# Splitting the first batch's keys and values by heads in an attention-plus-FFN kernel

## The chip, the cores and the metric

The kernel runs on one core of one Trainium2 chip. The metric is the device time of one execution in microseconds (us); the median of three runs before the change is 248.95 us (248.72 to 249.54). The traced execution of the same kernel spans 246.9 us from its first to its last instruction, and all times inside it below are counted from its start. Engines are named as in the profile: PE is the matrix engine (PEld its weight loads), DVE the vector engine, ACT the scalar engine, POOL the general-purpose engine that also issues most of the DMA transfers here, SP the engine that issues the others.

## The reference

A linear attention with cosine weights is followed by a feed-forward network with a product of two branches. There are 8 batches, 8 heads, 576 positions and a head dimension of 64:

```python
theta = pi / 2 * arange(576) / 576
phi(x) = concat([relu(x) * cos(theta), relu(x) * sin(theta)], axis=-1)     # 128 features
kv  = einsum('bhsf,bhsd->bhfd', phi(k), v)       # 128 x 64 for each head
z   = sum over s of phi(k)
num = einsum('bhsf,bhfd->bhsd', phi(q), kv)
den = einsum('bhsf,bhf->bhs', phi(q), z) + 1e-6
x   = (num / den), heads side by side            # 4608 tokens x 512
out = ((x @ w1) * (x @ w2)) @ w3 @ w_out         # 512 -> 1024 -> 1024 -> 512
```

All inputs and the output are 32-bit floats in DRAM; inside, the matrix products take bfloat16 operands and accumulate in 32 bits.

## The kernel before, in words

The product `w3 @ w_out` does not depend on the tokens, so the kernel forms it once (`w34b`, 1024 x 512) and then needs only three products for each token. Tokens are worked off in nine tiles of 512 columns. `ffn_groups(t)` is a generator that issues the matrix products of tile t in small groups and yields after each; after every yield the main loop runs whatever is listed in `slots[g]`, and so attention work of later batches is woven between the groups by hand. Nothing is moved by a scheduler (`tc.manual_schedule()`)[...].

The start is written out ahead of the loop, because nothing is there yet to be overlapped. For batch 0:

1. SP loads k as 32-bit floats (`load_first`, `load_first4` for the last 64 positions, "chunk 4"). POOL loads v, then q in two halves of two position chunks each, then the first column blocks of w1 and w2 (256 of 1024 columns a time, `load_w12`), casting to bfloat16 on the way. At most eight transfers of POOL's are under way: the ninth waits for the first one's completion.
2. DVE computes the cos and sin tables (`_trig_tables`), then the cos features of k in five chunks of positions; ACT computes the sin features; DVE copies v into `va`, whose last column is 1, so that the denominator comes out of the same product.
3. PE runs 27 products of zeros (`idle_mms`) while it waits, then `kv_first`: 40 products of 128 x 65, heads 0 to 3 in one PSUM bank, 4 to 7 in another. ACT copies both to `kvs`.
4. For a chunk c of 128 positions, `q_tr` turns the features of q on PE, ACT or DVE copies them out of PSUM (`qpT`), `num(0, c)` multiplies with `kvs`, DVE divides (`den`, `xblk`), `x_tr` turns the result on PE and DVE or ACT copies it into the columns of `xT` for tile 0. Chunks 0 and 1 are so treated ahead of the loop, chunks 2 and 3 from slots 1 and 3.

Tile 0 of the FFN begins as soon as chunk 0 is in `xT`. `on_half` treats columns 0 to 255, then 256 to 511; within a half, `pair` 0 and 1 are the hidden blocks 0-1 and 2-3 of w1 and w2. For `pair` 0 of half 0 and for all of half 1 the products are cut to 128 columns ("quarters"), so that they can begin before the second chunk of a half is there. `multiply` copies the w1 branch out of PSUM on ACT (`asb`) and multiplies it with the w2 branch on DVE (`abT`). Hidden blocks 4 to 7 follow with 512 columns each. Each block needs two PSUM banks out of four (`ffn_tile`, two pools of two).

Then come, still in tile 0, 16 groups that form `w34b`: for each 128-row block jp of w3, `w3_tr(jp)` turns it on PE, DVE copies it (`w3T`), and `w34_mm(jp, 0)` and `w34_mm(jp, 1)` multiply it with the first and second half of w_out. The order on PE around the first block is: `w3_tr(0)` (slot 13), hidden block 7, `w34_mm(0, 0)`, `w3_tr(1)` (slot 16), `w34_mm(0, 1)`. The weights for it are loaded by `other_loads`, which POOL begins once chunk 0's `xblk` is written: w2 and w1's remaining columns, w3 row block 0, w_out half 0, w3 block 1, w_out half 1, w3 blocks 2, 3, 4-5, then k of batch 1 and w3 blocks 6-7.

In the names of the profile, L462 is every product of `products` (the FFN's first layer), L532 the second layer, L237 `w34_mm`, L225 `w3_tr`, L336 and L349 turns of q, L417 `x_tr`, L365 `num`, L322 `kv_first`, L186 the products of zeros, L467/L468 `multiply`, L515/L519 the same for whole blocks.

Of the kernel before, what the change touches and what calls it, by code (L numbers as in the profile page):

```python
# [68 lines left out]
def kernel(  # L69
# [29 lines left out]
                                            space=bass.MemoryType.PSUM))  # L99
    first = [ctx.enter_context(ExitStack()) for _ in range(2)]  # L100
    ps_idle = first[1].enter_context(tc.tile_pool(name="ps_idle", bufs=1, space=bass.MemoryType.PSUM))
    ps_first = first[0].enter_context(tc.tile_pool(name="ps_first", bufs=1, space=bass.MemoryType.PSUM))

# [32 lines left out]
    def load_first4(eng, t, src, b=0):  # L136
        eng.dma_start(out=t[0:64, :, 4, :], in_=src[b, :, 512:S, :].rearrange("h p d -> p h d"))
# [16 lines left out]

    k0 = raw[0, "k"] = wst.tile([P, H, NCH, D], FP32, name="kf")
    q0 = raw[0, "q"] = ld.tile([P, H, NCH, D], BF16, name="qs", bufs=2)
    v0 = raw[0, "v"] = ld.tile([P, H, NCH, D], BF16, name="vs")
    load_first(nc.sync, k0, k)
    load_first4(nc.sync, k0, k)
    load_first(nc.gpsimd, v0, v)  # L160
    zeros = const.tile([P, 512], BF16, name="zeros")
    nc.vector.memset(zeros[:], 0.0)
    va_bufs, kp_bufs, qp_bufs = [], [], []

    def feature_buffers(i):

        va = const.tile([P, NCH, H, D + 2], BF16, name=f"va{i}")
        nc.vector.memset(va[:, :, :, D:D + 1], 1.0)
        nc.vector.memset(va[64:128, 4, :, 0:D], 0.0)
        va_bufs.append(va)  # L170
        for name, bufs in (("kp", kp_bufs), ("qp", qp_bufs)):
            fp = const.tile([P, NCH, H, F], BF16, name=f"{name}{i}")
            nc.vector.memset(fp[64:128, 4, :, :], 0.0)
            bufs.append(fp)

    feature_buffers(0)
    tiny = const.tile([P, 1], FP32, name="tiny")
    nc.scalar.activation(out=tiny[:], in_=zeros[:, 0:1], func=ACTF.Relu, scale=1.0, bias=0.0)

    unread = ps_idle.tile([P, 512], FP32, name="unread")  # L180
    kva = ps_idle.tile([P, 512], FP32, name="kva")

# [4 lines left out]

    idle_mms(27)
    cosv, sinv = _trig_tables(nc, const)
    identb = const.tile([P, P], BF16, name="identb")  # L190
    load_first4(nc.gpsimd, v0, v)
    load_first(nc.gpsimd, q0, q, 0, 2)
    make_identity(nc, identb[:])
    load_first(nc.gpsimd, q0, q, 2, 2)
    def load_w12(c0, n):
# [4 lines left out]
    load_w12(256, 256)  # L200
    load_first4(nc.gpsimd, q0, q)
    nc.gpsimd.dma_start(out=w1b[:, :, ds(512, 256)], in_=w1v[:, :, ds(512, 256)])

    def other_loads(behind):

        seen = sm.tile([P, 1], BF16, name="seen", bufs=1)
        nc.gpsimd.tensor_copy(out=seen[:], in_=behind)
        nc.gpsimd.dma_start(out=w2b[:, :, ds(512, 256)], in_=w2v[:, :, ds(512, 256)])
        load_w12(768, 256)
        for jp in range(2):  # L210
            load_w3(jp, 1)
            load_wout(jp)
        for jp in range(2, 4):
            load_w3(jp, 1)
        load_w3(4, 2)
        load(1, "k")
        load_w3(6, 2)
# [95 lines left out]

    def kv_first():

        kp, qp, va = feat[0]
        kvs = sm.tile([P, H, D + 1], BF16, name="kvs", bufs=2)
        kvb = ps_att.tile([P, 2, 512], FP32, name="pnum")
        halves = (kva[:, :], kvb[:, 0, :])
        for c in range(NCH):  # L320
            for h in range(H):
                nc.tensor.matmul(halves[h // 4][:, ds((h % 4) * 65, 65)], lhsT=kp[:, c, h, :],  # L322
                                 rhs=va[:, c, h, 0:D + 1], start=(c == 0 and h % 4 == 0),
                                 stop=(c == NCH - 1 and h % 4 == 3))
        att_of(0)["kvs"] = kvs
        yield
        for half in range(2):
            nc.scalar.copy(out=kvs[:, 4 * half:4 * half + 4, :], in_=halves[half][:, 0:260])
        yield

# [22 lines left out]
    def num(b, c, chain=True, in_two=False):  # L353
# [3 lines left out]
        qpT, kvs = att[b]["qpT"], att[b]["kvs"]  # L357
        if b == 0 and c == 0:
            nt = ps_first.tile([P, 2, 512], FP32, name="pfirst")
        else:  # L360
            pool = more_att[0] if more_att and order_of(b).index(c) % 2 == 0 else ps_att
            nt = None if in_two else pool.tile([P, 2, 512], FP32, name="pnum")
        banks = [ffn_tile(), ffn_tile()] if in_two else [nt[:, g, :] for g in range(2)]
# [92 lines left out]
    def ffn_groups(t):  # L456
# [14 lines left out]

        def on_half(half):

            if half == 1 and t == 0:
                banks = [(ffn_tile(), ffn_tile()) for _ in range(2)]
                for quarter in range(2):
                    for pair, (a, b) in enumerate(banks):
                        for i in range(2):
                            for ps, w in ((a, w1b), (b, w2b)):
                                products(ps[:, ds(256 * i + 128 * quarter, 128)], w, 2 * pair + i,  # L480
                                         ds(256 + 128 * quarter, 128))
                        if quarter == 1:
                            multiply(a, b, pair, half)
                        if quarter == 0 or pair == 1:
                            yield
                return
            for pair in range(2):
                a, b = ffn_tile(), ffn_tile()
                if pair == 0 and t == 0:
                    for quarter in range(2):  # L490
                        for i in range(2):
                            for ps, w in ((a, w1b), (b, w2b)):
                                products(ps[:, ds(256 * i + 128 * quarter, 128)], w, i,
                                         ds(256 * half + 128 * quarter, 128))
                            if half == 0 and quarter == 0 and i == 0:
                                yield
                        if quarter == 0:
                            yield
                else:
                    for ps, w in ((a, w1b), (b, w2b)):  # L500
                        for i in range(2):
                            products(ps[:, ts(i, 256)], w, 2 * pair + i, ts(half, 256))
                        if w is w1b and (t == 1 or half == 0):
                            yield
                multiply(a, b, pair, half)
                yield

        if t < 2:
            yield from on_half(0)
            yield from on_half(1)  # L510
        for jc in range(4 if t < 2 else 0, 8):
            aT = ffn_tile()
            products(aT[:, :], w1b, jc, slice(0, 512))
            asb = fsb.tile([P, 512], BF16, name="asb")
            nc.scalar.copy(out=asb[:], in_=aT[:, :])  # L515
            yield
            bT = ffn_tile()
            products(bT[:, :], w2b, jc, slice(0, 512))
            nc.vector.tensor_mul(out=abT[:, jc, :], in0=asb[:], in1=bT[:, :])  # L519
            yield  # L520
        if t == 0:
            for jp in range(8):
# [65 lines left out]

    for c in range(NCH):
        prep_k(0, c)  # L590
    for c in range(NCH):
        prep_v(0, c)
    kv_steps = kv_first()
    next(kv_steps)
    q0f = feat[0][1]
    features(0, q0f, q0, 0, scalar_heads=4)
    next(kv_steps)
    prep_q(0, 1)
    idle_mms(2)
    q_tr_halves(0, 0)  # L600
    prep_q(0, 2)
    idle_mms(1)
    num(0, 0)
    q_tr(0, 1, evac=False)[1]()
    other_loads(att[0]["x"][0][:, 0, 0, 0:1])
    features(0, q0f, q0, 3, sin=False)
    features(0, q0f, q0, 3, cos=False)
    idle_mms(2)
    x_tr(0, 0, by_vector=True)
    num(0, 1)  # L610
    q_tr(0, 2, evac=False)[1]()
    ps_ffn = []
    for stack in first:
        stack.close()
    for i in range(2):
        ps_ffn.append(ctx.enter_context(tc.tile_pool(name=f"ps_ffn{len(ps_ffn)}", bufs=2,
                                                     space=bass.MemoryType.PSUM)))


    at(1, lambda: x_tr(0, 1, by_vector=True), lambda: q_tr(0, 3, evac=False)[1](), lambda: num(0, 2))  # L620
    at(3, lambda: x_tr(0, 2), lambda: num(0, 3))
    at(5, lambda: x_tr(0, 3))
    at(6, lambda: features(0, q0f, q0, 4))
    at(23, lambda: transpose_q(0, 4))
# [72 lines left out]
```

## Time and profile before

| | |
|---|---|
| median of 3 runs | 248.95 us (248.72 to 249.54) |
| traced span | 246.9 us |
| PE busy | 240.5 us, 97% of the span |
| DVE, ACT, POOL busy | 135.9, 130.2, 93.4 us |
| DMA moved | 41.22 MB, mean 167 GB/s |
| waits of PE over 0.1 us after 1.2 us | five, together some 2 us, all before 34.1 us |

PE is busy in nearly every slice, so the span is PE's work plus the time in which PE has nothing useful to do. Such time lies only at the start: up to 10.11 us PE runs products of zeros or waits, and from there to 16 us it is used in part. To read the start, the timeline of single engines is more use than the sums: in it, each row has the start, the duration and, in brackets, the idle time before it and what ended that. A product's duration includes its drain, so products that follow one another without a gap overlap in the table by about 0.17 us.

### The profile page before, as it was taken

How to read it: one execution, taken by the hardware profiler on the slowest of the kernel's cores; microseconds unless marked ns; L12 is line 12 of the kernel's file. 1: busy time of each engine (PE TensorE's matmuls, PEld its weight loads, DVE VectorE, ACT ScalarE, POOL GpSimd, SP SyncE). 2: the span in 40 equal slices, each digit the busy share in tenths (PEclk: the TensorE clock that was granted, in tenths of full speed). 3: DMA queues.
4: the chain of work that ended last, by engine and by line, in shares of the span. 5: the costliest groups of instructions: out<-in, count | busy, mean ns of one | idle time of the engine just before them, and what ended most of it. 6: DMA issues, size and time to landing. Idle time of an engine off the chain costs nothing.

```text
span 246.9 us, 5034 instructions
## 1 busy us (share of the span) xinstructions
PE 240.5 (97%) x1872; PEld 130.4 (53%) x1872; DVE 135.9 (55%) x336; ACT 130.2 (53%) x266; POOL 93.4 (38%) x196
## 2 busy tenths in 40 slices
PE   8799999999999999999999999999999999999994
PEld 3479545566975445444544555454545554444443
DVE  7775652668968445647566475547464645312420
ACT  2676313767943873466556654854575333434332
POOL 7654342024512261127032612173322005978700
PEclk9999999999999999999999999999999999999999
DMA  7999999999999969999999999999994536998823
GB/s 199 178 194 199 201 207 204 198 181 173 153 162 142 167 100 149 132 149 134 169 144 155 118 180 150 150 140 140 166 142 89 94 64 214 260 281 289 282 101 128
DMA packets 86200, 41.22 MB, mean 167 GB/s; under 512 B 53792, under 2 KB 82720, under 8 KB 86176
## 3 DMA queue, kind: packets, MB, share of 16 engines
q0 software_dynamic: 37008, 27.20, 71.8%
q1 hardware_dynamic: 49168, 13.71, 35.9%
q8 instruction: 14, 0.23, 0.4%
q14 instruction: 10, 0.08, 0.1%
HBM read 38.80 MB, written 9.44 MB: 195 GB/s over the span
## 4 chain that ended last, share of the span: by engine, by line
PE 85%; DMA 10%; POOL 3%; issue 1%; ACT 0%; POOLq 0%
PE ffnps L462 45%; PE ffnps L532 24%; PE ffnps L237 6%; DMA woutb<-in_moe_w_out_dram 5%; DMA w2b<-in_moe_w_dram 5%; PE pnum L365 4%; PE pnum L305 4%; PE pst L225 1%; PE ffnps L548 1%; POOL qs L133 1%; POOL w1b L196 1%; PE pst L336 1%; POOL vs L133 0%; PE pst L417 0%; POOL w2b L197 0%
## 5 line engine op out<-in xcount | busy, mean ns | idle before, releaser
L462 PE MATMUL ffnps<-xT,w2b 128*128 128x512 bf16 (+2 forms) x344 | 75.5, 344 | 0.0
L462 PE MATMUL ffnps<-xT,w1b 128*128 128x512 bf16 (+2 forms) x344 | 75.5, 344 | 0.0
L519 DVE TENSOR_TENSOR abT<-asb,ffnps 128x512 bf16<-128x512 bf16 x64 | 43.9, 686 | 54.3 <-PE ffnps L462 52.4
L532 PE MATMUL ffnps<-w34b,abT 128*128 128x512 bf16 x280 | 65.0, 379 | 0.0
L515 ACT CAST asb<-ffnps 128x512 bf16<-128x512 f32 x64 | 37.4, 584 | 50.0 <-PE ffnps L462 45.2
L462 PEld LDWEIGHTS <-w2b 128*128 128x128 bf16 x344 | 31.0, 98 | 27.3
L462 PEld LDWEIGHTS <-w1b 128*128 128x128 bf16 x344 | 30.8, 98 | 25.9
L567 POOL COPY seen<-mark 1x1 bf16<-1x1 bf16 x50 | 8.9, 178 | 84.4 <-ACT mark L565 84.4
L532 PEld LDWEIGHTS <-abT 128*128 128x128 bf16 x280 | 26.0, 98 | 27.9 <-DVE abT L519 0.2
L539 ACT COPY osb<-ffnps 128x512 f32<-128x512 f32 x35 | 20.5, 584 | 35.2 <-PE ffnps L532 35.1
L274 ACT ACTIVATE qp<-qs,sinv 128x512 bf16<-128x512 bf16 (+2 forms) x40 | 28.1, 714 | 1.8 <-DMA qs<-in_q_dram 1.8
L383 DVE TENSOR_TENSOR xblk<-pnum,den 128x512 bf16<-128x512 f32 (+1 forms) x37 | 25.6, 691 | 1.3
L297 POOL COPY va<-vs 128x512 bf16<-128x512 bf16 (+1 forms) x30 | 17.6, 621 | 22.9 <-DMA vs<-in_v_dram 22.4
L274 ACT ACTIVATE kp<-ks,sinv 128x512 bf16<-128x512 bf16 (+1 forms) x35 | 25.0, 717 | 0.9 <-DMA ks<-in_k_dram 0.9
L447 POOL DMA_DIRECT2D out_dram<-osb x42 | 22.1, 531 | 2.7 <-issue 2.1
L365 PEld LDWEIGHTS <-qpT 128*128 128x128 bf16 x320 | 15.4, 98 | 8.7 <-DVE qpT L350 0.6
L381 DVE TENSOR_SCALAR den<-pnum 128x8 f32<-128x8 f32 (+1 forms) x37 | 6.0, 163 | 22.6 <-PE pnum L365 22.5
L237 PE MATMUL ffnps<-woutb,w3T 128*128 128x512 bf16 x64 | 15.8, 380 | 0.2 <-DMA woutb<-in_moe_w_out_dram 0.2
L365 PE MATMUL pnum<-kvs,qpT 128*128 128x65 bf16 x296 | 15.8, 194 | 0.0
L270 DVE TENSOR_SCALAR qp<-qs,cosv 128x512 bf16<-128x512 bf16 (+1 forms) x40 | 15.3, 389 | 0.7 <-DMA qs<-in_q_dram 0.7
L305 PEld LDWEIGHTS <-kp 128*128 128x128 bf16 x280 | 11.4, 98 | 4.1
L270 DVE TENSOR_SCALAR kp<-ks,cosv 128x512 bf16<-128x512 bf16 (+1 forms) x35 | 12.5, 367 | 0.0
(88 smaller groups left out, 181.6 us busy)
## 6 DMA issues: line engine op xcount, KB each, us to landing
out_dram<-osb POOLq DMA_DIRECT2D x16, 256.0 KB, 4.5
out_dram<-osb POOLq DMA_DIRECT2D x24, 128.0 KB, 3.9
qs<-in_q_dram POOLq DMA_DIRECT2D x8, 256.0 KB, 7.6
ks<-in_k_dram POOLq DMA_DIRECT2D x6, 320.0 KB, 6.3
qs<-in_q_dram POOLq DMA_DIRECT2D x6, 320.0 KB, 5.9
vs<-in_v_dram POOLq DMA_DIRECT2D x6, 320.0 KB, 5.7
ks<-in_k_dram POOLq DMA_DIRECT2D x6, 256.0 KB, 7.0
vs<-in_v_dram POOLq DMA_DIRECT2D x6, 256.0 KB, 5.4
```

The lines of the kernel that those rows point to most:

```text
L237: nc.tensor.matmul(acc[:, :], lhsT=w3T[:, lc, :], rhs=woutb[:, lc, :], start=(lc == 0), stop=(lc == 7))
L270: nc.vector.tensor_scalar(out=dst[:R, c, :, 0:D], in0=src[:R, :, c, :], scalar1=0.0, scalar2=cosv[:R, at:at + 1], op0=ALU.max, op1=ALU.mult)
L274: nc.scalar.activation(out=dst[:R, c, 0:n, D:F], in_=src[:R, 0:n, c, :], func=ACTF.Relu, scale=sinv[:R, at:at + 1], bias=0.0)
L305: nc.tensor.matmul(kvt[:, h // 4, ds((h % 4) * 65, 65)], lhsT=kp[:, c, h, :], rhs=va[:, c, h, 0:D + 1], start=(i == 0 and h % 4 == 0), sto ...
L365: nc.tensor.matmul(banks[h // 4][:, ds((h % 4) * 65, 65)], lhsT=qpT[:, h, ds(at, 128)], rhs=kvs[:, h, :], start=True, stop=True)
L383: nc.vector.tensor_tensor(out=xblk[rows, g], in0=n4[:, :, :, 0:D], in1=den[rows, g].unsqueeze(3).to_broadcast([R, G, 4, D]), op=ALU.mult)
L447: eng.dma_start(out=rows[:, :, cols], in_=osb[64 * i:64 * i + rows.shape[0], :, cols])
L462: nc.tensor.matmul(out, lhsT=w[:, kc, ts(jc, 128)], rhs=x[:, kc, tok], start=(kc == 0), stop=(kc == 3))
L515: nc.scalar.copy(out=asb[:], in_=aT[:, :])
L519: nc.vector.tensor_mul(out=abT[:, jc, :], in0=asb[:], in1=bT[:, :])
L532: nc.tensor.matmul(ops[:, :], lhsT=abT[:, jc, ts(ms, 128)], rhs=w34b[:, jc, :], start=(jc == 0), stop=(jc == 7))
L539: nc.scalar.copy(out=osb[:, ms % 2, :], in_=ops[:, :])
```

## The change

The idea is to let the first work begin on half of the data. k and v of batch 0 are loaded by halves of the heads; the features, the `kv` product, its copy and the numerator of chunks 0 and 1 are then done for heads 0-3 while heads 4-7 are still on their way. In order:

- k's heads 0-3 are loaded by SP as 32-bit floats, k's chunk 4 into a tile of its own (`k4`); k's heads 4-7 by POOL, cast to bfloat16. v is loaded in two halves by POOL, the second after k's second half. The integer tables for cos and sin go ahead of POOL's first transfer.
- The zero fills of `kp` and `va` for the missing 64 rows go from DVE to ACT; that of `qp` is put off to slot 6.
- `kv_first` is replaced by `first_kv(half)`, `num(0, 0)` and `num(0, 1)` by `first_num(c, half)`. 17 products of zeros stay of 27, and two of the later five.
- Tile 0 of the FFN no longer goes half by half but chunk by chunk for hidden blocks 0-1 (`chunk`), with blocks 2-3 of the first half between chunks 2 and 3, and of the second half after block 4 (`first_tile`). `x_tr(0, 2)` is moved to slot 2, `num(0, 2)` to slot 0.
- In `other_loads` both halves of w_out go ahead of w3 block 1, and q's chunk 4 is loaded after it, where before it went ahead of w1's third block.

The diff, cut to what bears on the order of work:

```diff
-    load_first(nc.sync, k0, k)
-    load_first4(nc.sync, k0, k)
-    load_first(nc.gpsimd, v0, v)
+    load_half(nc.sync, k0[0], k, 0, slice(0, 4))
+    nc.sync.dma_start(out=k4[0:64, :, :], in_=k[0, :, 512:S, :].rearrange("h p d -> p h d"))
...
+    cosv, sinv = _trig_tables(nc, const)
+    load_half(nc.gpsimd, v0, v, 0, slice(0, 4))
...
-    idle_mms(27)
-    cosv, sinv = _trig_tables(nc, const)
-    identb = const.tile([P, P], BF16, name="identb")
+    idle_mms(17)
     load_first4(nc.gpsimd, v0, v)
     load_first(nc.gpsimd, q0, q, 0, 2)
+    load_half(nc.gpsimd, k0[1], k, 1, slice(0, 4))
+    identb = const.tile([P, P], BF16, name="identb")
     make_identity(nc, identb[:])
+    load_half(nc.gpsimd, v0, v, 1, slice(4, 8))
     load_first(nc.gpsimd, q0, q, 2, 2)
...
     load_w12(256, 256)
-    load_first4(nc.gpsimd, q0, q)
     nc.gpsimd.dma_start(out=w1b[:, :, ds(512, 256)], in_=w1v[:, :, ds(512, 256)])
...
-        for jp in range(2):
-            load_w3(jp, 1)
-            load_wout(jp)
+        load_w3(0, 1)
+        for half in range(2):
+            load_wout(half)
+        load_w3(1, 1)
+        load_first4(nc.gpsimd, q0, q)
...
+        def first_tile():
+            banks = [(ffn_tile(), ffn_tile()) for _ in range(2)]
+            for c in range(4):
+                if c == 3:
+                    yield from on_half(0, 1)
+                yield from chunk(*banks[c // 2], c)
+                if c % 2:
+                    multiply(*banks[c // 2], 0, c // 2)
+                yield
+            yield from whole(4)
+            yield from on_half(1, 1)
...
+    first_keys(0)
+    first_values(0)
+    first_kv(0)
     q0f = feat[0][1]
-    features(0, q0f, q0, 0, scalar_heads=4)
-    next(kv_steps)
+    prep_q(0, 0)
     prep_q(0, 1)
     idle_mms(2)
     q_tr_halves(0, 0)
-    prep_q(0, 2)
-    idle_mms(1)
-    num(0, 0)
+    first_keys(1)
+    halves = [first_num(0, 0)]
     q_tr(0, 1, evac=False)[1]()
-    other_loads(att[0]["x"][0][:, 0, 0, 0:1])
...
+    first_values(1)
+    halves[0]()
+    features(0, q0f, q0, 2, sin=False)
+    first_kv(1)
+    halves.append(first_num(1, 0))
+    halves.append(first_num(0, 1))
+    halves[1]()
+    halves[2]()
+    features(0, q0f, q0, 2, cos=False)
+    q_tr(0, 2, evac=False)[1]()
+    other_loads(att[0]["kvs"][:, 4, 0:1])
+    halves.append(first_num(1, 1))
+    x_tr(0, 0, by_vector=True)
+    halves[3]()
...
-    at(1, lambda: x_tr(0, 1, by_vector=True), lambda: q_tr(0, 3, evac=False)[1](), lambda: num(0, 2))
-    at(3, lambda: x_tr(0, 2), lambda: num(0, 3))
-    at(5, lambda: x_tr(0, 3))
-    at(6, lambda: features(0, q0f, q0, 4))
+    at(0, lambda: num(0, 2))
+    at(1, lambda: x_tr(0, 1), lambda: q_tr(0, 3, evac=False)[1]())
+    at(2, lambda: x_tr(0, 2, by_vector=True), lambda: num(0, 3))
+    at(4, lambda: x_tr(0, 3))
+    at(6, lambda: nc.vector.memset(qp_bufs[0][64:128, 4, :, :], 0.0))
+    at(19, lambda: features(0, q0f, q0, 4))
```

The changed kernel has the same 40 slots in tile 0, so everything from slot 7 on, and all of tiles 1 to 8, is issued in the order of before.

## The prediction

> **What bounds the kernel now.** I read the page first, then the waits of PE, then PE's timeline from 0 to 36 us, then the DMA issues one by one, and last the chain of waits.
>
> ```profile
> PE 240.5 (97%) x1872; PEld 130.4 (53%) x1872; DVE 135.9 (55%) x336; ACT 130.2 (53%) x266; POOL 93.4 (38%) x196
> PE   8799999999999999999999999999999999999994
> DMA  7999999999999969999999999999994536998823
> ```
>
> PE is busy everywhere but at the start, and DMA is full from the start to about 85 us. Only the start can give time, and there PE and DMA both have a claim. PE's timeline (start, duration, what it did; overlapping durations mean no gap):
>
> ```profile
> 1.20 7.74 PE L186 MATMUL unread<-zeros 128*128 128x512 bf16 x27 [1.20 <-DVE zeros L162]
> 10.11 0.29 PE L322 MATMUL kva<-va,kp 128*128 128x65 bf16 x4 [1.18 <-DVE va L297]
> ...
> 15.01 0.40 PE L417 MATMUL pst<-identb,xblk 128*128 128x128 bf16 x4 [0.34 <-DVE xblk L383]
> 15.34 0.43 PE L365 MATMUL pnum<-kvs,qpT 128*128 128x65 bf16 x8
> 15.61 0.61 PE L336 MATMUL pst<-identb,qp 128*128 128x128 bf16 x8
> 16.05 0.39 PE L462 MATMUL ffnps<-xT,w1b 128*128 128x128 bf16 x4
> 16.27 0.39 PE L462 MATMUL ffnps<-xT,w2b 128*128 128x128 bf16 x4
> ...
> 33.23 0.61 PE L225 MATMUL pst<-identb,w3b 128*128 128x128 bf16 x8
> 34.02 1.89 PE L237 MATMUL ffnps<-woutb,w3T 128*128 128x512 bf16 x8 [0.18 <-DMA woutb<-in_moe_w_out_dram]
> ```
>
> Tile 0 of the FFN starts at 16.05. From there to `w3_tr(1)` at 33.23 no row has an idle time: 17.18 us without a gap. Then PE waits 0.18 us for w_out's second half and is never held up by more than 0.1 us again. So the time is fixed by when PE starts `w34_mm(0, 1)`: 34.02 now. All that follows is the same work in the same order, and I forecast the shift of that start.
>
> Landings follow from the DMA view of single issues (size as written, median time to landing), with the issue times of POOL's timeline:
>
> ```profile
> w1b<-in_moe_w_dram POOLq DMA_DIRECT2D x1, 256.0 KB, 8.5
> w2b<-in_moe_w_dram POOLq DMA_DIRECT2D x1, 256.0 KB, 9.1
> ```
>
> Issued at 5.92 and 6.66, these land at 14.4 and 15.8, so tile 0 begins just 0.3 us after w2's first block. In the same way v lands at 9.8, its chunk 4 at 10.3, q's halves at 11.7 and 13.0, w1's and w2's second blocks at 17.1 and 19.6. A block of 512 KB of 32-bit source takes 1.35 to 1.40 us. Near the end of the list:
>
> ```profile
> 20.43 13.55 DMA woutb<-in_moe_w_out_dram
> 34.02 1.89 PE ffnps L237 x8
> ```
>
> This is from the chain of waits: w_out's second half lands at 33.98. PE and DMA arrive there together.
>
> [...] SP's k (32 bits written) moves at 373 to 393 GB/s, POOL's casting loads write some 195 GB/s, which is 390 GB/s read. [...] v's issue ended at 2.32, yet POOL's queue moved nothing before 5.25, when SP's k was nearly through. [...] products of zeros start every 0.43 us up to 4.9 us, then about every 0.21. [...]
>
> **The change part by part.**
>
> *Loads.* Before w2's first block lie k, v, q's two halves and w1's first block, as before, so the block lands at 15.8 again; it only has a different order ahead. Counting 1.36 us back per block from the landings of before: k's first half 5.2, v's first half 7.05 and chunk 4 7.55, q's first half 8.95, k's second half 10.3, v's second 11.66 (the place q's first half had), q's second 13.0.
>
> *Until the FFN starts.* The cos and sin tables start about 1 us earlier (POOL's integer tables take 0.5 us and no longer stand behind a 1.04 us issue; 1.2 us of fills are gone from DVE), so at 5.1 DVE is ready as k's half lands. `first_kv(0)` ends near 8.3 instead of 11.4, q's chunks 0 and 1 are turned by 11.4. But the last data decides: v's second half at 11.66; four DVE copies, about 0.15 each for half of the columns (0.24 full): 12.3; `first_kv(1)` ends 12.8. ACT is late: from k's second half at 10.3, four sin features at 0.41 each (the 128x256 one took 0.51 with 0.1 overlapped) to 12.1, the qpT copy of 1.01 to 13.0, kvs to 13.3. `first_num(0, 1)` ends at 13.6. On DVE, cos for q's chunk 2 (0.35) and two normalizations of 0.8 (den 0.15, reciprocal 0.18, xblk 0.42 and the gaps between) end at 15.0. `x_tr` 0.4, xT copy 0.42: the FFN starts at 15.93, against 16.05. Ten products of zeros fewer, three fills fewer and 0.7 us saved on `kv` all go into waiting. PE has by then done the same attention work as before (`kv`, turns of chunks 0 to 2, both numerators), so 0.12 us is gained.
>
> *Tile 0 by chunks.* The number of products stays: 16 groups of four with 128 columns at 0.2235 and eight with 256 at 0.44 make 7.10 us, against 24 and four, 7.12. What changes is distance. Before, between a chunk's `x_tr` and its use stood at least 0.7 us of other products. Three uses now follow too closely:
>
> 1. Chunk 1. `x_tr(0, 1)`, then only `q_tr(0, 3)`, 0.44 us. xT is copied by ACT, 0.58. Drain 0.17, hand-overs 0.04 and 0.05 (17.39 to 17.42 in the trace of before): 0.84 - 0.44 = 0.40 us of waiting.
> 2. Chunk 2. The code issues chunk 1's `multiply` first and then `x_tr(0, 2)`, whose copy is on DVE. [...] the copy stands behind the product, which stands behind ACT's `asb`. From chunk 1's last product: drain 0.17, `asb` 0.58, product 0.69 less the 0.07 by which DVE's neighbours overlap, copy 0.42, hand-overs 0.15: 1.94. Beside it PE has `x_tr(0, 2)` and `num(0, 3)`, 0.22 and 0.26. Wait: 1.46 us.
> 3. Block 4. Chunks 2 and 3 use the pool's two banks that block 4 needs next. `asb` of chunk 3 must be copied first: drain 0.17, 0.05, 0.58, 0.05: 0.85 us with nothing between. Before, 0.9 us of products lay there.
>
> Sum 2.71 us. Behind each stands the whole of PE's queue.
>
> *The end of tile 0's first layer.* 15.93 + 17.16 + 2.71 = 35.80 for `w3_tr(1)`, 36.24 for `w34_mm(0, 1)`: 2.22 us after 34.02.
>
> *w_out ahead of w3 block 1, q's chunk 4 later.* `w34_mm(0, 1)` needs w_out's second half and, since PE's order is fixed, w3 block 1 ahead of it. All that lands before both is the same but for q's chunk 4 (128 KB, 0.35 us): 33.6 instead of 33.98. At 35.8 both are there; the 0.18 us wait is gone, which is in the sum. It can bring no more, since PE is late. q's chunk 4, prepared in slot 19, is turned by DMA: ACT's part ends near 40, and the same transfer took 9.2 us in before (issued 23.68); it would be there near 49, and `num(0, 4)` is due at 48.41 + 2.2. No wait.
>
> *Nothing else.* The fills on ACT (three of 0.58) lie before 4 us, where ACT waits for k anyway; that in slot 6 (0.48) fits where DVE waited 2.2 us. The remaining edits only change which pool a PSUM tile comes from.
>
> Forecast: 248.95 + 2.2 = 251.1 us.
>
> **The rivals.**
>
> *DMA-bound, same time.* If the three waits were hidden, PE would reach `w3_tr(1)` at 33.1 and wait for w3 block 1 until 33.6; plus 0.44 it starts `w34_mm(0, 1)` at 34.05: 249.0. For it: PE and DMA meet at 34 us. Against: the waits follow from the code's order and from durations in the trace. A part of them hidden gives 249.7 to 250.5.
>
> *Faster.* The handover from SP's to POOL's transfers, where the rate falls from 380 to 130-150 instead of 195 GB/s for about 1 us, would have to go, and with it q's chunk 4: 33.0 + 0.44, and no wait at all on PE: 248.3, and with a stream faster by half a microsecond more, 247.9. Against it: nothing loads less.
>
> *Late or cold start, slower still.* POOL's first transfer is issued some 0.6 us later than now. If its queue could not move before 5.5 us for reasons of its own, not because SP's stood ahead, DMA would stand idle from 4.2 on and all landings move by 1.3: 252.4. Against it: at 204.23, with DMA idle, a store of POOL's moved bytes after 1.0 us. Or PE, with some 40% of work from 8.5 to 16 us, goes back to half clock[...].
>
> **How the numbers follow.** All three waits, about as worked out (250.5 to 252): 0.58. Partly hidden (249.7 to 250.5): 0.10. Late or cold: 0.12. DMA-bound, same: 0.12. Faster: 0.08. Slower by over 0.3% (over 249.7) is 0.58 + 0.10 + 0.12 = 0.80; same 0.12; faster 0.08. The range leaves out the faster case, the lower part of the same and the upper part of the late ones: 249.2 to 252.6.
>
> **What would show it.** In the profile after, PE's waits should hold three new ones: an FFN product on ACT's xT (0.4), one on DVE's xT (1.5), one on ACT's `asb` (0.85). The FFN's first product at 15.9, w2's first block landing at 15.8, `w34_mm(0, 1)` near 36.2 without a wait on DMA. A first FFN product before 15 us, or PE without gaps from there to 33 us, would make the forecast wrong; products at double length near 16 us would show the cold clock, and no bytes of POOL's between 4.2 and 5.5 the late start.

## The result and the profile after

The changed kernel is slower: 250.65 us (250.56 to 250.99, 6 executions) against 249.53 us for the kernel before in the same comparison, ratio 1.0050 [1.0030, 1.0071]. A larger comparison later gave 251.28 against 249.27, ratio 1.0078 [1.0055, 1.0101]. So the change costs 1.1 to 2.0 us; the traced span grew from 246.9 to 249.0 us.

The page of the kernel after, engines and slices:

```profile
PE 236.7 (95%) x1814; PEld 129.3 (52%) x1843; DVE 137.1 (55%) x347; ACT 132.7 (53%) x273; POOL 96.2 (39%) x198
PE   8478999999999999999999999999999999999994
DMA  7999999999989999999999899989995436898923
```

PE's row shows less work in the second to fourth slice (6 to 25 us), and nothing later. (The lower count of products is partly the 13 missing products of zeros and partly records that the trace lacks.) The waits of PE from 16 to 36 us, in the kernel after:

```profile
PE ffnps L512 <- DVE xT L469: 1.5, 2, 1.0
PE ffnps L512 <- ACT asb L517: 0.5, 1, 0.5
PE ffnps L512 <- ACT xT L469: 0.2, 1, 0.2
```

These are the three names of the forecast, besides tile 0's own start (0.52 of the 1.5 us). Before, this stretch had only 0.2 us on w_out. PE's timeline of the kernel after gives their places:

```profile
16.43 0.38 PE L512 MATMUL ffnps<-xT,w1b 128*128 128x128 bf16 x4 [0.52 <-DVE xT L469]
...
17.80 0.61 PE L389 MATMUL pst<-identb,qp 128*128 128x128 bf16 x8
18.64 0.38 PE L512 MATMUL ffnps<-xT,w1b 128*128 128x128 bf16 x4 [0.23 <-ACT xT L469]
...
19.75 0.42 PE L415 MATMUL pnum<-kvs,qpT 128*128 128x65 bf16 x8
21.20 0.38 PE L512 MATMUL ffnps<-xT,w1b 128*128 128x128 bf16 x4 [1.02 <-DVE xT L469]
...
24.73 0.39 PE L512 MATMUL ffnps<-xT,w2b 128*128 128x128 bf16 x4
25.56 1.02 PE L512 MATMUL ffnps<-xT,w1b 128*128 128x512 bf16 x3 [0.45 <-ACT asb L517]
...
35.60 0.61 PE L239 MATMUL pst<-identb,w3b 128*128 128x128 bf16 x8
36.05 1.34 PE L251 MATMUL ffnps<-woutb,w3T 128*128 128x512 bf16 x5
```

The idle time in brackets counts from the modelled end of the drain. The time lost in PE's queue is longer by most of the drain, here 0.16 to 0.17 us: eight turns take 0.44, so after 17.80 the next group could start at 18.24 and starts at 18.64, 0.40 lost. In the same way 21.20 - (19.75 + 0.26) = 1.19 and 25.56 - (24.73 + 0.22) = 0.61. Sum 2.20 us. The work between is 35.60 - 16.43 - 2.20 = 16.97 us, close to the 17.18 of before. `w34_mm(0, 1)` starts at 36.05, 2.03 us after before's 34.02, with no wait on DMA.

### The profile page after: what moved, and what is told of

Same layout as the page of the kernel before. It is cut to its first block, busy times and chain, and to the rows that moved or that the text cites. A ratio compares the mean times of both kernels' runs of the same rounds, so it can differ in the third digit from the quotient of the medians.

```text
span 249.0 us, 4972 instructions
## 1 busy us (share of the span) xinstructions
PE 236.7 (95%) x1814; PEld 129.3 (52%) x1843; DVE 137.1 (55%) x347; ACT 132.7 (53%) x273; POOL 96.2 (39%) x198
## 4 chain that ended last, share of the span: by engine, by line
PE 90%; DMA 3%; POOL 2%; DVE 2%; ACT 1%; issue 1%; POOLq 0%
PE ffnps L512 49%; PE ffnps L583 24%; PE ffnps L251 5%; PE pnum L415 4%; PE pnum L319 4%; DMA qs<-in_q_dram 3%; PE pst L239 1%; PE ffnps L599 1%; PE pst L467 1%; POOL vs L158 1%; PE pst L389 1%; ACT asb L517 0%; POOL qs L133 0%; ACT qpT L392 0%; DVE xblk L379 0%
## 5 line engine op out<-in xcount | busy, mean ns | idle before, releaser
L512 PE MATMUL ffnps<-xT,w1b 128*128 128x512 bf16 (+2 forms) x323 | 73.5, 347 | 2.7 <-DVE xT L469 1.5
L583 PE MATMUL ffnps<-w34b,abT 128*128 128x512 bf16 x270 | 63.6, 379 | 0.5
L288 ACT ACTIVATE qp<-qs,sinv 128x512 bf16<-128x512 bf16 (+1 forms) x40 | 28.3, 719 | 0.1
L433 DVE TENSOR_TENSOR xblk<-pnum,den 128x512 bf16<-128x512 f32 (+1 forms) x36 | 24.9, 691 | 1.2
L415 PEld LDWEIGHTS <-qpT 128*128 128x128 bf16 x304 | 14.8, 98 | 8.1
L284 DVE TENSOR_SCALAR qp<-qs,cosv 128x512 bf16<-128x512 bf16 (+1 forms) x40 | 16.9, 432 | 1.0 <-DMA qs<-in_q_dram 0.9
L284 DVE TENSOR_SCALAR kp<-ks,cosv 128x512 bf16<-128x512 bf16 (+1 forms) x35 | 12.5, 367 | 1.4 <-DMA ks<-in_k_dram 1.4
```

The costliest lines, as they stand in the source:

```text
L284: nc.vector.tensor_scalar(out=dst[:R, c, :, 0:D], in0=src[:R, :, c, :], scalar1=0.0, scalar2=cosv[:R, at:at + 1], op0=ALU.max, op1=ALU.mult)
L288: nc.scalar.activation(out=dst[:R, c, 0:n, D:F], in_=src[:R, 0:n, c, :], func=ACTF.Relu, scale=sinv[:R, at:at + 1], bias=0.0)
L415: nc.tensor.matmul(banks[h // 4][:, ds((h % 4) * 65, 65)], lhsT=qpT[:, h, ds(at, 128)], rhs=kvs[:, h, :], start=True, stop=True)
L433: nc.vector.tensor_tensor(out=xblk[rows, g], in0=n4[:, :, :, 0:D], in1=den[rows, g].unsqueeze(3).to_broadcast([R, G, 4, D]), op=ALU.mult)
L512: nc.tensor.matmul(out, lhsT=w[:, kc, ts(jc, 128)], rhs=x[:, kc, tok], start=(kc == 0), stop=(kc == 3))
L583: nc.tensor.matmul(ops[:, :], lhsT=abT[:, jc, ts(ms, 128)], rhs=w34b[:, jc, :], start=(jc == 0), stop=(jc == 7))
```

## The experiments

The theory: three waits in tile 0, made by the order chunk by chunk, cost the time. The rivals: the later start (loads, thinner PE work), the clock, the order of w_out. Ratios are to the kernel before in the same comparison. "Clock" is the share of full speed that the profile shows as granted to PE; the figure for an execution is its mean.

**The kernel before once more**, and two hybrids that cross the change's halves: the new start with the old tile 0, and the old start with the new tile 0. The fourth kernel below shared the chip with them.

> The kernel before, unchanged, as a second trace. In its first trace the second half of the first w3 x w_out block starts at 34.02 us and the span is 246.9 us; the timed runs of before went from 248.7 to 250.2 us. Theory (the loss is all in tile 0): the ratio to before is 1.000, and the start of that product is again near 34.0, so the trace of after is 2.0 us behind. Rival (the first trace of before was a fortunate one, and the loss is nearer 1.1 us): the product starts at 34.5 to 35.0 and the trace shows where.

Measured: 248.93 us (12 executions) against 249.07 (29), ratio 0.9996 [0.9971, 1.0022]. In this trace `w34_mm(0, 1)` starts at 33.48, earlier than either forecast, and without a wait on w_out; the span, 247.2 us, is still 0.3 longer than in the first trace. So single traces of one kernel differ by 0.5 us at this point.

```diff
 # the changed kernel, with tile 0's first layer and its slots put back
-            yield from first_tile()
+        if t < 2:
+            yield from on_half(0)
+            yield from on_half(1)
...
-    at(0, lambda: num(0, 2))
-    at(1, lambda: x_tr(0, 1), lambda: q_tr(0, 3, evac=False)[1]())
-    at(2, lambda: x_tr(0, 2, by_vector=True), lambda: num(0, 3))
-    at(4, lambda: x_tr(0, 3))
+    at(1, lambda: x_tr(0, 1, by_vector=True), lambda: q_tr(0, 3, evac=False)[1](), lambda: num(0, 2))
+    at(3, lambda: x_tr(0, 2), lambda: num(0, 3))
+    at(5, lambda: x_tr(0, 3))
```

> The changed kernel's start and loads, with tile 0 in the order of before (half by half, x_tr and num in their old slots). Theory: the loss is the three waits in tile 0 (0.40, 1.19 and 0.61 us in the trace after). They go: PE has no gap from the FFN's first product (16.4) to w3_tr(1), which starts near 33.5, and the product with w_out's second half starts at 33.9 to 34.1; time 2.0 us under the changed kernel's, ratio to before 1.000 within 0.002. Rival: the new start with its later landings (w2's first block 0.6 us later) costs as much; then the time stays 1 us or more above before, with the FFN's first product or DMA waits late.

Measured: 249.66 us, ratio 1.0030 [1.0009, 1.0050]. PE's timeline of this kernel:

```profile
16.33 0.38 PE L512 MATMUL ffnps<-xT,w1b 128*128 128x128 bf16 x4 [0.51 <-DVE xT L469]
...
33.36 0.61 PE L239 MATMUL pst<-identb,w3b 128*128 128x128 bf16 x8
33.81 1.99 PE L251 MATMUL ffnps<-woutb,w3T 128*128 128x512 bf16 x8
```

From 16.33 to 33.36 no row has an idle time: 17.03 us of pure work, and `w34_mm(0, 1)` is 2.24 us earlier than in the kernel after. The start of the FFN is as late as there.

The time is not quite back: the ratio lies above the 1.000 within 0.002 that was expected. Three of the 12 executions had a clock of 0.993; the other nine have a median of 249.33, still 0.26 us over before. So the new start has a small cost of its own.

The other hybrid is the same swap on the kernel before (the diff above reversed).

> The kernel before with only tile 0's order of the changed kernel (chunk by chunk, x_tr and num in the new slots); loads and start as before. Theory: the FFN starts at 16.0 as before, the three waits come (0.4, 1.2, 0.6), and the product with w_out's second half starts at 36.0; time 1.5 to 2.2 us over before, ratio 1.006 to 1.009. Rival (the start is to blame): time within 0.5 us of before.

Measured: 251.34 us, ratio 1.0096 [1.0063, 1.0129]. Its timeline of PE:

```profile
17.41 0.43 PE L365 MATMUL pnum<-kvs,qpT 128*128 128x65 bf16 x8 [0.66 <-ACT qpT L339]
19.19 0.38 PE L462 MATMUL ffnps<-xT,w1b 128*128 128x128 bf16 x4 [0.23 <-ACT xT L419]
21.81 0.38 PE L462 MATMUL ffnps<-xT,w1b 128*128 128x128 bf16 x4 [1.08 <-DVE xT L419]
26.17 1.02 PE L462 MATMUL ffnps<-xT,w1b 128*128 128x512 bf16 x4 [0.45 <-ACT asb L467]
```

The three waits come with the order of tile 0 and without the new start, at the same sizes (0.23, 1.08, 0.45). A fourth, 0.66, comes because here `num(0, 2)` in slot 0 meets a qpT that the old start copies later. This is the main verdict: the order of tile 0 carries most of the loss. The time is 2.27 us over before, more than the changed kernel's 1.1 to 2.0, as is to be expected with a fourth wait.

**The copy ahead of the multiply.** Only the longest wait is attacked: chunk 2's turn and DVE copy are issued before chunk 1's `multiply`.

```diff
                 yield from chunk(*banks[c // 2], c)
+                if c == 1:
+                    x_tr(0, 2, by_vector=True)
                 if c % 2:
                     multiply(*banks[c // 2], 0, c // 2)
...
-    at(2, lambda: x_tr(0, 2, by_vector=True), lambda: num(0, 3))
+    at(2, lambda: num(0, 3))
```

> The changed kernel with one thing moved: x_tr of chunk 2 is issued right after chunk 1's products and ahead of its multiply, so that DVE copies xT before it multiplies. Theory: the 1.19 us wait before chunk 2 falls to about 0.4 (transpose, drain and copy 0.85, less num's 0.26 and the transposes' 0.22), all else stays: the product with w_out's second half starts near 35.3 instead of 36.05, time 0.7 to 0.8 us under the changed kernel's. Rival (ACT or the landing of data holds chunk 2, and the order on DVE doesn't matter): no change.

DVE's queue in the kernel after, where the copy is behind the product, and the product behind ACT's `asb`:

```profile
20.12 0.69 DVE L518 TENSOR_TENSOR abT<-asb,ffnps 128x512 bf16<-128x512 bf16 x1 [1.66 <-ACT asb L517]
20.73 0.42 DVE L469 COPY xT<-pst 128x512 bf16<-128x512 bf16 x1
```

Chunk 2's turn on PE ends at 19.92 (19.53 and 0.39), and DVE is idle from 18.46 to 20.12; still the copy starts only behind the product, in the order of the code. With the copy first it starts at 20.26 in a trace whose FFN began at 16.74, and PE's timeline has

```profile
20.06 0.42 PE L415 MATMUL pnum<-kvs,qpT 128*128 128x65 bf16 x8
20.74 0.38 PE L512 MATMUL ffnps<-xT,w1b 128*128 128x128 bf16 x4 [0.25 <-DVE xT L469]
```

The loss falls from 1.19 to 20.74 - (20.06 + 0.26) = 0.42 us. From the FFN's first product to `w34_mm(0, 1)` it takes 18.85 us, after it took 19.62: 0.77 less, as expected. The time doesn't show it: 251.03 us, ratio 1.0079 [1.0055, 1.0103]. Here the FFN started 0.3 us later, and two of eight executions had a clock of 0.992; but the other six have a median of 250.95 too, so the clock is not the reason. The trace is 0.46 us ahead of the changed kernel's at `w34_mm(0, 1)` (35.59), and only 0.1 at its end (span 248.9 against 249.0). So this run shows that the order on DVE's queue made the wait, and does not show a gain in time.

**The kernel after once more**, with more executions.

> The changed kernel, unchanged, as a second trace and a second comparison with before. Theory (PE's waits in tile 0 set the loss): the product with w_out's second half starts 19.6 us after the FFN's first product again, near 36.0, with waits of 0.4, 1.2 and 0.6 us in between; time 1.1 to 2.0 us over before. Rival (the first comparison was off): outside of that.

Measured: 251.28 us (20 executions), 1.0078 [1.0055, 1.0101]. Five of the 20 had a clock of 0.993 and took 251.9 to 253.2 us; the 12 at full clock had a median of 250.9 (the highest of them 252.1, so the clock doesn't make the whole spread). The traced one is one of the five. PE's timeline:

```profile
17.59 0.62 PE L512 MATMUL ffnps<-xT,w1b 128*128 128x128 bf16 x4
...
20.26 0.39 PE L512 MATMUL ffnps<-xT,w1b 128*128 128x128 bf16 x4
```

and its windows, each a microsecond; after the length come busy time of PE, PEld, DVE, ACT and POOL, then the granted clock, DMA share and GB/s:

```profile
16.00:17.00 1.00, 0.61 (x7) 0.60 (x7) 0.93 (x5) 0.76 (x2) 1.00 (x3) 0.75 1.46 197
17.00:18.00 1.00, 1.00 (x16) 1.00 (x14) 0.83 (x3) 0.00 (x0) 0.62 (x2) 0.50 1.49 209
...
20.00:21.00 1.00, 1.00 (x20) 0.92 (x17) 0.00 (x0) 1.00 (x2) 0.37 (x1) 1.00 1.45 196
```

A group of four products that takes 0.39 us at full clock takes 0.62 here. The clock is halved at about 16.5 and is back by 20, after a stretch in which PE was busy some 60% of the time. No idle time between 8 us and there was longer than 0.65 us. `w34_mm(0, 1)` starts at 37.41, 1.36 us later than in the first trace of this kernel. (Another 1.08 us of this trace's 251.4 is a wait on a transposing DMA at 81.83 us.) The first trace of this kernel, at full clock throughout, was no busier before, and had an idle time of 1.50 us ahead of 8.02. The same stretch in both, this one first:

```profile
8.00:16.40 8.40, 5.30 (x87) 3.88 (x87) 6.63 (x29) 6.43 (x13) 5.30 (x9) 1.00 1.52 191
8.00:16.40 8.40, 5.30 (x86) 3.86 (x86) 6.47 (x28) 6.44 (x12) 5.28 (x9) 1.00 1.54 193
```

So the share of busy time doesn't decide alone whether the clock falls: of two executions with 63%, one fell.

**The order of the weights alone.** The kernel before, with w_out ahead of w3 block 1 and q's chunk 4 behind it.

```diff
     load_w12(256, 256)
-    load_first4(nc.gpsimd, q0, q)
...
-        for jp in range(2):
-            load_w3(jp, 1)
-            load_wout(jp)
+        load_w3(0, 1)
+        for half in range(2):
+            load_wout(half)
+        load_w3(1, 1)
+        load_first4(nc.gpsimd, q0, q)
...
-    at(6, lambda: features(0, q0f, q0, 4))
+    at(19, lambda: features(0, q0f, q0, 4))
```

> The kernel before with nothing changed but the order of the weights: both halves of w_out ahead of w3 block 1, q's chunk 4 behind it (its features in slot 19). Theory (the same data must land before the product with w_out's second half, whichever comes first): w3 block 1 lands near 33, PE is at w3_tr(1) near 33.2, the product starts between 33.5 and 34.0; time within 0.5 us of before. Rival (w_out earlier frees PE at 34 us): 0.5 us or more under before. Second rival (q's chunk 4 comes too late): a wait of PE for qpT before num(0, 4) near 48 us and a time above before.

Measured: 249.07 us (20), 0.9987 [0.9969, 1.0005]: no difference from before. `w3_tr(1)` is followed by `w34_mm(0, 1)` at 33.27 without a wait on w_out; but the second trace of before has none either, so this is not shown to come from the order. Nor does PE wait for q's chunk 4 near 48 us.

**Tile 0 spread.** Hidden blocks 2-3 of the first half go between chunks 1 and 2, so that other products lie between each copy and its use.

```diff
-            banks = [(ffn_tile(), ffn_tile()) for _ in range(2)]
             for c in range(4):
-                if c == 3:
+                if c == 2:
                     yield from on_half(0, 1)
-                yield from chunk(*banks[c // 2], c)
+                if c % 2 == 0:
+                    banks = (ffn_tile(), ffn_tile())
+                yield from chunk(*banks, c)
```

> The changed kernel with hidden blocks 2-3 of the first half moved from between chunks 2 and 3 to between chunks 1 and 2, and the banks of chunks 2 and 3 taken only then. Theory: with 1.76 us of products ahead of chunk 2 its copy is in time (1.19 us gone), and block 4 gets banks that have been read long since (0.61 us gone); the wait for chunk 1 stays (0.40) and one of about 0.4 us for chunk 3's xblk comes. The product with w_out's second half starts 18.2 us after the FFN's first product instead of 19.6; time 1.2 to 1.5 us under the changed kernel's. Rival (DMA holds PE at w3 block 1): less than 0.7 us.

Measured: 250.40 us (12), 1.0038 [1.0008, 1.0069]. PE's timeline from 16 us holds these waits:

```profile
16.24 0.38 PE L512 MATMUL ffnps<-xT,w1b 128*128 128x128 bf16 x4 [0.52 <-DVE xT L469]
18.45 0.38 PE L512 MATMUL ffnps<-xT,w1b 128*128 128x128 bf16 x4 [0.23 <-ACT xT L469]
22.04 0.40 PE L467 MATMUL pst<-identb,xblk 128*128 128x128 bf16 x4 [0.32 <-DVE xblk L433]
```

The waits for chunk 2 and block 4 are gone, a short new one on xblk came. `w34_mm(0, 1)` starts at 34.55, 18.31 us after the FFN's start. Five of 12 executions had a clock of 0.986 to 0.993; the other seven have a median of 249.66, 1.2 us under the 250.9 of the changed kernel at full clock in the same comparison, as expected.

**k's chunk 4 first.** The new start with the old tile 0, with SP's two loads of k swapped, to see whether the late landings come from the small pieces of chunk 4 at the end of SP's queue.

> As the run with the new start and tile 0's old order, but SP loads k's chunk 4 (256-byte pieces) ahead of k's heads 0-3. In that run POOL's casting stream wrote only 106 to 164 GB/s from 4.5 to 7 us, beside the tail of chunk 4, and w2's first block landed at 16.3 instead of 15.4 to 15.8 before. Theory (the tail of small pieces slows the casting stream): the rate is 180 to 195 GB/s from 5 us on, w2's block lands by 15.8, the FFN starts near 15.9, time 0.3 to 0.5 us under that run. Rival (the casting stream begins slowly in any case, or k's second half as a cast is the cause): w2's block at 16.2 or later, no gain.

Measured: 250.78 us (20), 1.0048 [1.0019, 1.0076]. The loads didn't land earlier (w2's first block at 16.97). But SP's queue was no sooner done: k's heads 0-3, now its second load, landed only at 7.9. So the run doesn't tell whether a rest of SP's transfers slows the beginning of POOL's. And PE had nothing to do:

```profile
10.38 0.80 PE L358 MATMUL pnum<-va,kp 128*128 128x65 bf16 x17 [3.51 <-DVE va L345]
```

Its clock then fell to about half, as the third digit of the page's row of granted clock shows (12.5 to 18.7 us); 13 of 20 executions had a clock of 0.985 to 0.993, and the seven at full clock a median of 249.21, level with before's 249.27:

```profile
PEclk9959999999999999999999999999999999999999
```

**The gaps filled.** Ten more products of zeros between 9 and 16.4 us, where PE waits in any case: in the kernel after, in the new start with the old tile 0, and in the spread tile 0.

```diff
-    idle_mms(2)
+    idle_mms(5)
     q_tr_halves(0, 0)
...
+    idle_mms(2)
     first_kv(1)
+    idle_mms(1)
...
     halves.append(first_num(0, 1))
+    idle_mms(2)
...
     x_tr(0, 0, by_vector=True)
+    idle_mms(2)
```

> The changed kernel with ten more products of zeros, put where PE waits between 9 and 16.4 us (three before the turn of q's chunk 0, two before first_kv(1), one and two around the numerators, two before the FFN). In the second set of the changed kernel 5 of 20 executions, the traced one among them, had a mean granted PE clock of 0.993 and took 251.9 to 253.2 us, the trace with products at half rate from 16.4 to 19.7 us; those at 1.000 had a median of 250.9; before had none of 63 below 0.998. Theory (PE's thin work from 9 to 16 us lets the clock fall back in some executions): with the fill none is below 0.998, the upper tail above 251.9 goes, median 250.7 to 250.9 with the waits in tile 0 unchanged. Rival (the clock falls for another reason): still about a quarter at 0.993.

Measured: 250.80 us (5), 1.0085 [1.0064, 1.0106]; the three waits of tile 0 are unchanged.

> The new start with tile 0's old order, and the same ten products of zeros. Without them it had a median of 249.66, with 3 of 12 executions at 0.993 (250.0 to 250.4) and the others around 249.3. Theory: with the waits and the clock falls both gone it is level with before, ratio 0.999 to 1.002; the new start gains nothing, since the FFN's first product stands at 16.3. Rival (the halves by heads are a gain once undisturbed): ratio under 0.998.

Measured: 249.62 us (21), 1.0023 [1.0006, 1.0039]; no wait in tile 0, `w34_mm(0, 1)` at 33.73.

> The changed kernel with hidden blocks 2-3 between chunks 1 and 2 (two of the three waits gone, one of 0.3 new), and the ten products of zeros. Without them 5 of 12 executions were at 0.986 to 0.993 (250.7 to 251.5), the others around 249.7. Theory: none below 0.998, median near 249.6, that is some 0.4 us over before. Rival: still above 250.2.

Measured: 249.91 us (12), 1.0036 [1.0018, 1.0055].

None of the 38 executions had a clock below 0.998. Over all runs the clock was below 0.995 in none of 211 executions of kernels with the old start, and in 15 of 58 of those with the new start, unfilled, apart from the kernel with k's chunk 4 first. From 8.0 to 16.4 us PE is busy for 5.30 to 5.49 us in the traces of the unfilled new start, for 6.52 and 6.89 in the two of before, and for 7.34 to 7.45 in those of the filled kernels. So the lower clock goes with the new start's thin stretch. (The three filled kernels ran on one chip and the unfilled ones on others; side by side on one chip they were not measured.)

The filled kernels also give the cost of tile 0's order at full clock: 250.80 - 249.62 = 1.2 us. The spread tile 0 wins back 250.80 - 249.91 = 0.9 of it, by two of the three waits. The remaining 249.62 - 248.95 = 0.7 us over before is the new start's own, ratio 1.0023 where at most 1.002 was expected. From the executions at full clock it was 0.3 without the filler, and nothing with k's chunk 4 first, so its size stays open.

**An earlier load of k of batch 3.** In the traces of the kernel before once more and of the order of the weights alone, small later waits on loads and on transposing DMAs took back what PE was ahead. This kernel, the one with the new order of the weights, loads batch 3's k some slots earlier.

```diff
-    plan_loads(3, (36, 37, 47, 50, 54, 57))
+    plan_loads(3, (36, 37, 44, 46, 54, 57))
```

> The kernel before with the new order of the weights (w_out ahead of w3 block 1) and, besides, the load of batch 3's keys in slots 44 and 46 instead of 47 and 50. In the second trace of before, DVE waited 0.74 us for these keys at 79 us, a product of the FFN stood behind it on DVE, and PE waited 0.53 us; before's executions at full clock spread from 248.2 to 250.9 us. Theory (late waits for such loads make up that spread): that wait is gone, the median falls to 248.6 or 248.8 against 249.0 to 249.3 of before, ratio 0.997 to 0.999. Rival (the spread has other causes): ratio 0.999 to 1.001.

Measured: 249.63 us (22) against 248.74, ratio 1.0030 [1.0015, 1.0046]: slower, so this theory falls. The waits of PE for DMA in this kernel:

```profile
75.62 0.43 PE L366 MATMUL pnum<-kvs,qpT 128*128 128x65 bf16 x8 [0.45 <-DMA qpT<-qp]
78.03 0.43 PE L366 MATMUL pnum<-kvs,qpT 128*128 128x65 bf16 x8 [0.25 <-DMA qpT<-qp]
...
181.20 1.04 PE L463 MATMUL ffnps<-xT,w1b 128*128 128x512 bf16 x4 [1.47 <-DMA xT<-xblk]
```

DVE no longer waits for batch 3's k. Instead PE waits at 75.62 and 78.03 for transposing DMAs, soon after the earlier load, which is issued from 68.28 to 70.33 (from 71.16 to 74.84 with the order of the weights alone). That the load delays them is likely, not shown. The longest wait comes 100 us later and has no visible link to the load; the order of the weights alone waits 0.18 us at the same product.

No kernel of these is faster than the one before; the nearest, the new order of the weights alone, is level with it.

## Why the prediction was right, and where it was off

- **The three waits.** Right, and shown: they appear with the new tile 0 in either start and are absent with the old tile 0 in either start. The second shrinks when its copy is issued earlier, and the second and third go when other products are put between.
- **Their sizes.** Forecast 0.40, 1.46, 0.85; lost in the queue 0.40, 1.19, 0.61. The first is exact. The other two are each some 0.25 too long by one term: the drain from which `asb` waits was counted from the chunk's last group. `asb` copies the bank of w1 alone, whose last group ends one group, 0.22 us, before the last of w2. ACT's timeline of the kernel after has it beside PE's last w2 group of chunk 3 (24.73 to 25.12):

```profile
24.93 0.59 ACT L517 CAST asb<-ffnps 128x512 bf16<-128x512 f32 x1 [0.47 <-PE ffnps L512]
```

- **The start of the FFN.** Forecast 15.93, came at 16.43 (16.2 to 16.7 in other traces of the new start, but for the one with k's chunk 4 first). The step "the block lands at 15.8 again" failed: v's second half landed at 12.3 instead of 11.66, and w2's first block at 16.39. The block is not what held the FFN, since its first product stands at 16.65. PE waited for DVE's xT, and DVE was late from q's first half on:

```profile
9.60 0.80 DVE L284 TENSOR_SCALAR qp<-qs,cosv 128x512 bf16<-128x512 bf16 x2 [0.87 <-DMA qs<-in_q_dram]
...
15.95 0.42 DVE L469 COPY xT<-pst 128x512 bf16<-128x512 bf16 x1 [0.38 <-PE pst L467]
```

  The q that DVE waits for was forecast for 8.95. v's half landed just as DVE had finished the features of k's second half (at 12.35), so which of the two came last can't be told. All these landings are late by some 0.6 us: the loads move the same bytes, but the casting stream of POOL's queue begins slowly. In the kernel after, from 4.5 us, DMA wrote 139 GB/s over all queues; over as long a stretch after the handover in the kernel before, 171:

```profile
4.50:7.00 2.50, 2.02 (x10) 0.79 (x9) 1.45 (x5) 1.71 (x4) 2.39 (x6) 1.00 1.26 139
```

```profile
5.75:8.25 2.50, 2.50 (x13) 1.17 (x12) 2.04 (x6) 1.59 (x3) 2.50 (x5) 1.00 1.44 171
```

  Why it begins slowly stays open.
- **The sum.** 0.50 later at the start and 0.51 less of waits cancel, and 0.2 less work leaves +2.03 for the forecast +2.22. So the shift is near by luck of two errors of opposite sign. The time lies in the range with less luck: 1.1 us over before in the first comparison and 2.0 in the larger one, for a forecast of 2.2.
- **"All that follows is the same work."** True of the first pair of traces: the span grew by 2.1 us for +2.03. But it isn't a law. The second execution of before was 0.5 us ahead at `w34_mm(0, 1)` (33.48), and waited later for k of batch 3. The filled new start with the old tile 0 was 0.29 ahead of before there, and its span is 0.3 longer. Its list of waits has nothing later, for it leaves out single idle times under 0.15 us; the timelines show where the lead went. The largest piece, before first and then the filled kernel:

```profile
78.46 1.89 PE L532 MATMUL ffnps<-w34b,abT 128*128 128x512 bf16 x8
80.18 0.42 PE L365 MATMUL pnum<-kvs,qpT 128*128 128x65 bf16 x8
```

```profile
78.39 2.13 PE L582 MATMUL ffnps<-w34b,abT 128*128 128x512 bf16 x8
80.36 0.42 PE L415 MATMUL pnum<-kvs,qpT 128*128 128x65 bf16 x8
```

  The same eight products take 1.97 us to the next row instead of 1.72; DVE's `abT` starts at 79.41 instead of 79.10, behind a feature of batch 3's k that took 0.51 instead of 0.33, and PE's weight loads wait 0.6 us for it instead of 0.2. Two smaller steps, at 65.54 and 132.57, lose 0.14 and 0.11; together 0.50 of the 0.59 us. Why they come is open, and so is how far they make the 0.7 us of the medians; the kernel before itself spreads over 248.1 to 251.2 us at full clock.
- **w_out ahead of w3 block 1.** Right: no measurable difference alone.
- **The rivals.** The late start of POOL's queue did not occur: its first bytes moved between 4.0 and 4.5 us, with no dead stretch. (That POOL's queue has to wait for SP's, as the late first bytes in the kernel before could suggest, is not shown: with k's chunk 4 first, both moved at once, from 4.5 to 7.0 us 0.20 MB for SP and 0.27 for POOL.) The cold clock shared 0.12 with the late start: a mean clock of 0.993 occurs in 5 of 20 executions of the larger comparison, and the fall costs 1.36 us up to `w34_mm(0, 1)` where it was traced. The share of work was also forecast too low, at 40% instead of 63%. What makes the clock fall was not shown: in the trace in which it fell no idle time from 8 us on was over 0.65 us, and the first trace, with the same 63% and an idle time of 1.50 us, kept full clock. The clock is not the cause of the median, since the filled kernel, whose clock was never below 0.998, has the same loss.

## What to carry to other kernels

When work is cut into smaller pieces, look at the distance in each engine's queue between each copy and its use. Here a copy that feeds PE, issued ahead of a product that doesn't, cut a wait from 1.19 to 0.42 us (without a gain in time that could be shown), and with other products between the reading of two banks and their reuse a wait of 0.61 was gone. An earlier first piece brought nothing here, where the last loads and the work behind them set the start: the FFN began at 16.43 us against 16.05. And where a change thins PE's work, keep its filler products: here the mean clock was below 0.995 in 15 of 58 executions without them (in the traced one of them the clock halved with no idle time over 0.65 us ahead of it) and in none of 38 with them, on another chip.

## What the hardware showed that was not expected

- PE's clock fell to half for about 3.4 us (16.5 to 19.9) after a stretch of 63% work, without an idle time over 0.65 us from 8 us on, in a traced execution whose mean clock was 0.993. The mean was below 0.995 in about a quarter of the executions of the unfilled new start (15 of 58). With ten products of zeros in the gaps it was so in none of 38, on another chip.
- POOL's queue moved its first bytes at 5.25 us in the kernel before and between 4.0 and 4.5 after, although its first transfer was issued by 2.3 in before: in both it began when SP's load was nearly through (1.04 of 1.18 MB moved by 5.25 us; 0.57 of 0.66 by 4.0 and 0.63 by 4.5).
- A lead or a shift of half a microsecond at 34 us need not reach the end: in the traces here it was lost in later waits of 0.1 to 0.5 us, on DVE's `abT` behind a feature of k and on transposing DMAs.
